# Attention into an ELU feed-forward layer: the first 64 queries of a pair of heads as float16 halves turned by a DMA

## The chip, the cores and the metric

The kernel runs on one core of a Trainium2 chip. The metric is device time in microseconds, the median of several executions. Engines are named as the profile names them: PE is TensorE (PEld its weight loads), DVE VectorE, ACT ScalarE, POOL GpSimd, SP SyncE, which issues all loads and stores.

## The reference

```python
scores = (1/8) * q @ k.T                        # batch 8, heads 8, sequence 576, head size 64
cum    = cumsum(max(s, 0))
scores = where(causal, -1e9, scores + min(-(cum_i - cum_j), 0))
attn   = softmax(scores)
x      = (attn @ v), heads side by side         # 4608 x 512
h      = x @ w_in                               # 512 x 2048
g      = where(h > 0, h, exp(min(h, 0)) - 1)
out    = g @ w_out                              # 4608 x 512, float32
```

## The kernel before, in words

Attention and the feed-forward layer run interleaved in one program. The sequence of 576 queries is cut into the first 64 and four blocks of 128 (`NQ` = 4, `HB` = 64). Heads are worked on in pairs: four pairs in each of the eight batches. The order of the work is: batches 0 to 2, the first 64 queries and blocks 0 and 1, in float32 (class `Low`); batch 3, the same queries, in float16 parts; batches 4 to 7, all queries; at last batches 0 to 3, blocks 2 and 3. The feed-forward layer takes the results in chunks of 256 rows, 18 in all, the first in float32 and the others as products of float16 parts (`moe_chunk`).

Where an operand is split, it is a scaled float16 high part and a float16 rest; a product is three matmuls: high by high, rest by high, high by rest.

A `Unit` is one step of attention. For the five batches 3 to 7 each pair of heads has three units: `h` = None, which does the first 64 queries of both heads at once (one block of 128 x 128: 64 queries of either head against 64 keys of either head, the cross blocks masked away), then `h` = 0 and `h` = 1 for the blocks of each head. So there are 20 units with `h` = None. The pairs of the last batches 0 to 3 have none.

Before, a unit with `h` = None goes like this. `prepare` rounds the 64 values of both heads to float32r and takes the rest (L416, L437). `scoring` makes the scores, the exponentials and their sums (L1065, L1068, L1073), and `normalize` multiplies by the inverse sum (L1086 to L1090). `weighing` turns the block on PE (L1218), copies it out of PSUM in two float32r parts (L443 or L444, L1151) and multiplies both with the values (L1211, two matmuls of 128 columns). The result has 128 rows (high and rest of the values) that are added up by `halves`: for each head a copy (L443 or L444) and an addition (L1280), into the columns 0 to 63 of the tile `x`.

The units with `h` = 0 and 1 do the same for their blocks with float16 parts: `halved` scales the probabilities into a high part and a rest (L1125 to L1133), a transposing DMA (`turned_load`, L409) turns them, and the products of the two heads are issued together after the second (`heads`, L1252). Each of these matmuls has 64 columns of values as weights (128*64 in the profile) and writes one half of the rows of the PSUM bank `av`, head 0 one half and head 1 the other. One eviction with a scale brings the bank into `x` (L1264 on ACT or L1266 on DVE), and a store takes `x` to `x_dram`, from where the feed-forward chunks load it (L404).

PSUM has eight banks: two of the tag "a" (scores and turned blocks), one "av", three "h" and one each of "o0" and "o1" for the feed-forward layer. `any_bank` asks for a bank of "a" or "av". The tile `x` has one buffer (`N_X` = 1).

The order on every engine is written by a planner (`Plan`). An operation lists the engines that could do it with an estimated cost each, what it reads and what it writes. `issue` takes again and again the operation that could start first by the estimates (the smaller priority number in a tie) and puts it on the engine where it would end first. The order is then fixed: each engine executes its instructions in that order, whatever the true durations are. For a buffer with several possible banks it takes the bank that came free earliest:

```python
for key, bufs, *rule in b.others:
    other = slot_free(key, bufs)
    if other is not None and (at is None or other < at):
        at, b.key, b.bufs = other, key, bufs
```

Of the kernel before, what the change touches and what calls it, by code (L numbers as in the profile page):

```python
# [8 lines left out]

F32 = mybir.dt.float32  # L10
F32R = mybir.dt.float32r
U32 = mybir.dt.uint32
BF16 = mybir.dt.bfloat16
F16 = mybir.dt.float16
# [3 lines left out]
P = 128  # L18
# [337 lines left out]
def kernel(  # L356
# [52 lines left out]
        op(prio, [("SP", SP_TURN, lambda: nc.sync.dma_start_transpose(dst(), src()), LAG,  # L409
                   units * P * P * 2)], reads, writes)  # L410

    def rounded(prio, n, dst, src, reads, writes, sign=1.0, only=None):

        ways = [
            ("Pool", pool_1(n),
             lambda: pool.tensor_scalar(dst(), src(), sign, 1.0, ALU.mult, ALU.mult)),  # L416
            ("ACT", act_s(n),
             lambda: act.activation(dst(), src(), AF.Copy, scale=sign)),
            ("DVE-SB", dve_1(n),
             lambda: dve.tensor_scalar(dst(), src(), sign, None, ALU.mult)),  # L420
        ]
        op(prio, [w for w in ways if only is None or w[0] in only], reads, writes)

    def scaled(prio, n, dst, src, by, reads, writes):

        op(prio, [
# [3 lines left out]
            ("DVE-SB", 220 + 0.7 * n, lambda: dve.tensor_scalar(dst(), src(), by(), None, ALU.mult)),  # L430
        ], reads, writes)

    def rest(prio, n, dst, src, hi, reads, writes, only=None):

        ways = [
            ("DVE-SB", dve_2(n), lambda: dve.tensor_tensor(dst(), src(), hi(), ALU.subtract)),
            ("Pool", pool_2(n), lambda: pool.tensor_tensor(dst(), src(), hi(), ALU.subtract)),  # L437
        ]
        op(prio, [w for w in ways if only is None or w[0] in only], reads, writes)

    def psum_copy(prio, n, dst, src, reads, writes, only=None):
        ways = [
# [578 lines left out]
    def prepare(u):  # L1021

        if u.h == 1 or (u.h == 0 and not u.blocks[0]):
            return
        turn = pairs_seen[0] % 2
        pairs_seen[0] += 1
        if len(pair_sets) == turn:
            pair_sets.append(plan.buf(sb, [P, 4, 2, S], F16, "set_1", tag=w_all[1].key[1]))
        if pairs_seen[0] <= 2:
            weigh(pair_sets[turn])  # L1030
        u.set = pair_sets[turn]
        prepare_pair(u, u.set)
        if u.h is not None:
            return
        b, j, prio = u.b, u.j, u.prio
        u.vs = plan.buf(sb, [P, 1, 2, D], F32R, f"vs_{u.tag}", tag="vs0", bufs=NP)
        if u.col == 4:
            prio = PRIO_V
        src, used = (lambda: u.va.v[:, j, :1]), values_of(u.va, j)
        rounded(prio, D, lambda: u.vs.v[:, :1, 0], src, used, [u.vs])  # L1040
        rest(prio, D, lambda: u.vs.v[:, :1, 1], src,
             lambda: u.vs.v[:, :1, 0].bitcast(F32), used, [u.vs])

    plan.signal = (id(ps), "o0")

# [99 lines left out]
            turned_load(prio, turns, lambda: u.pt.v[:, at::n][:, :turns],  # L1145
                        lambda: t16.v[:, base * P : (base + turns) * P], used, [(u.pt, i)])

    def split_pt(prio, tag, tr, w):
        pc = plan.buf(sb, [P, 2, w], F32R, f"pc_{tag}", tag="pc")
        psum_copy(prio, w, lambda: pc.v[:, 0], lambda: tr.v[:, :w], [tr], [(pc, 0)])  # L1150
        op(prio, [("DVE", dve_p(w), lambda: dve.tensor_tensor(  # L1151
            pc.v[:, 1], tr.v[:, :w], pc.v[:, 0].bitcast(F32), ALU.subtract))],
           [tr, (pc, 0)], [(pc, 1)])
        return [(pc, 0), (pc, 1)]

    def scoring(u):

        prio = u.prio
# [5 lines left out]
        used = [(o, part) for part in ("top", "low", "q2", "aux", "weights")]  # L1164
        if u.h is None:
            sm = plan.buf(sb, [P, 1], F32, f"sm_{u.tag}", tag="sm", bufs=2)
            psh = u.pp = plan.buf(sb, [P, P], F32, f"psh_{u.tag}", tag="pc")

            def pair():
                softmax_block(  # L1170
                    prio, u.tag, False, psh, P, masks,
                    lambda at, w: masks.v.rearrange("p h t -> p (h t)"), used,
                    lambda at, w: [
                        (row(q, S - HB, 2 * HB), row(k, u.first, 2 * (S - u.first)).rearrange(
                            "p (h t) -> p h t", h=2)[:, :, :HB]) for q, k in ((Q1, K1), (Q2, K2))],
                    (sm, 0, True, 1, 1.0), view=lambda v: v.rearrange("p (h t) -> p h t", h=2),
                )
                normalize(prio, psh, P, sm, 0)

            return [pair]  # L1180
        c0 = HB * (u.blocks[0] == 0)
# [21 lines left out]
    def weighing(u):  # L1203

        prio = u.prio + 1
        av = plan.buf(ps, [P, 512], F32, f"av_{u.tag}", tag="av", bufs=N_AV)

        def products(cost, pairs, dst, first, last):

            for m, (reads, operands) in enumerate(pairs):  # L1210
                op(prio, [("PE", cost, lambda m=m, operands=operands: pe_.matmul(  # L1211
                    av.v[:, dst], *operands(), start=first and m == 0,
                    stop=last and m == len(pairs) - 1))], reads, [av])

        if u.h is None:
            def pair():
                tr = plan.buf(ps, [P, 512], F32, f"tr_{u.tag}", tag="a", bufs=N_A)
                op(prio, [("PE", 111.0, lambda: pe_.transpose(tr.v[:, :P], u.pp.v, ident))],  # L1218
                   [(u.pp, "data")], [tr])
                pieces = split_pt(prio, u.tag, tr, P)  # L1220
                products(pe(P), [
                    ([pc, u.vs], lambda pc=pc, m=m: (
                        u.vs.v.rearrange("p n a d -> p n (a d)")[:, 0], pc[0].v[:, m]))
                    for m, pc in enumerate(pieces)], slice(P), True, True)
                for h in range(2):
                    halves(prio, h, HB, u.x_part((h, 0)), 0, av, h * HB)

            return [pair]

        if u.h == 0:  # L1230
            return []
        pair = (u.first_head, u)
        first, last, wq = u.blocks[0], u.last + 1, P * u.n_blocks

        def columns(kb):
            i0, half = max(kb - 1, first), kb > first
            return P * (last - i0) - HB * half

        def part(w, kb, m):
            c = columns(kb)  # L1240
            if kb == last:
                return w.pt.v[:, 0, P - c :]
            end = (1 + (2 * kb + m + 1) * w.n_blocks) * P
            return w.pt.v.rearrange("p u q -> p (u q)")[:, end - c : end]

        def heads():
            def step():
                for kb in range(last + 1):
                    dst = slice(wq - columns(kb), wq)
                    for m, v in ((0, 0), (1, 0), (0, 1)) if kb < last else ((0, 0), (0, 1)):  # L1250
                        for w in pair:
                            pe_.matmul(  # L1252
                                av.v[w.h * HB : (w.h + 1) * HB, dst], w.values.v[:, w.h, kb, v], part(w, kb, m),
                                start=kb == 0 and m == 0 and v == 0, stop=kb == last and v == 1,
                            )
# [5 lines left out]
            x, label = u.x_part(("rows", first))  # L1261
            back, cols = slice(u.back, u.back + 1), slice(HB + P * first, HB + P * first + wq)
            op(prio, [
                ("ACT", act_c(wq) + 90, lambda: act.activation(  # L1264
                    x.v[:, cols], av.v[:, :wq], AF.Copy, scale=scales.v[:, back])),
                ("DVE", dve_p(wq), lambda: dve.tensor_scalar(  # L1266
                    x.v[:, cols], av.v[:, :wq], scales.v[:, back], None, ALU.mult)),
            ], [av, (scales, u.back)], [(x, label)])
# [5 lines left out]
    def halves(prio, h, n, dst, c0, av, a0):  # L1274

        x = dst[0]
        own, other = slice(h * HB, (h + 1) * HB), slice((1 - h) * HB, (2 - h) * HB)
        cols, here = slice(c0, c0 + n), slice(a0, a0 + n)
        psum_copy(prio, n, lambda: x.v[own, cols], lambda: av.v[other, here], [av], [dst])
        op(prio, [("DVE", dve_p(n), lambda: dve.tensor_tensor(  # L1280
            x.v[own, cols], av.v[own, here], x.v[own, cols], ALU.add))], [av], [dst])

    def attention():

# [15 lines left out]
        for u, prepared, scored, weighed in todo:  # L1300
# [5 lines left out]
            if type(u) is Unit and u.h is not None:  # L1306
# [1 line left out]
                    pair = pair_values(u, *values)  # L1308
                u.values, u.back = pair, values[1] + 1
                if u.h == 0:  # L1310
                    first_head = u
                u.first_head = first_head
            prepared(u)
            if type(u) is Unit and not hasattr(u, "set"):
                u.set, u.first = operands
# [337 lines left out]
```

## Time and profile before

| | |
|---|---|
| median of 3 runs | 1038.81 us (1037.28 to 1039.48) |
| the profiled execution | 1034.6 us, span 1032.8 us |
| mean granted clock of PE | 0.996 |
| busy PE, PEld | 1003.1 us (97%), 688.7 us (67%) |
| busy DVE, ACT, POOL | 845.2 us (82%), 669.0 us (65%), 295.9 us (29%) |
| transposing DMAs | 168 |
| half-width matmuls (L1252) | 960 |
| float32 turns and products of the first 64 queries (L1218, L1211) | 20 and 40 |

The span is from the first to the last instruction. A busy time is the union of an engine's instructions. Matmuls overlap in the profile, so what one adds to the time of PE is read from the distance of the starts, not from its duration. In a row of a group the last numbers are busy us, mean ns of one, and then the idle time just before with what ended it.

### The profile page before, as it was taken

Reading aid. Unit: us, or ns where it says so; the run is one execution under the profiler, and the core shown is the slowest. Engines: PE = TensorE matmul, PEld = TensorE weight load, DVE = VectorE, ACT = ScalarE, POOL = GpSimd, SP = SyncE. Lnnn points to the kernel's source line nnn. Section 1 sums busy time; section 2 is a strip of 40 time slices with the busy share of each in tenths; the row PEclk is TensorE's granted clock in tenths of the full one; section 3 lists DMA queues with packets and bytes.
Section 4 is the critical chain, followed back from the end, with each engine's and each line's share of the span. In section 5 each row is a group of like instructions: output and inputs, shape, how many; then the busy total and the mean of one; then the engine's idle time right before and its main releaser. Section 6 shows DMA issues by size and latency. Waiting matters only on the chain. (4 is left out here: it accounts for less than half of the span.)

```text
span 1032.8 us, 21782 instructions
## 1 busy us (share of the span) xinstructions
PE 1003.1 (97%) x7305; PEld 688.7 (67%) x7305; DVE 845.2 (82%) x2346; ACT 669.0 (65%) x1559; POOL 295.9 (29%) x487
## 2 busy tenths in 40 slices
PE   8889999999999999999999999999999999999998
PEld 6667656676666666666666666676666676666665
DVE  7999998788988988898889999798988898863232
ACT  4898755666667766776776766666675765644343
POOL 6343452242323323241234242222232123100000
PEclk9999999999999999999999999999999999999999
DMA  7997524589979997999989987979998998841000
GB/s 197 276 289 236 150 72 95 124 190 213 222 166 212 207 192 165 198 202 208 196 174 201 232 179 174 229 181 192 215 198 196 227 202 187 182 94 47 1 21 21
DMA packets 296724, 179.83 MB, mean 174 GB/s; under 512 B 209908, under 2 KB 270564, under 8 KB 296612
## 3 DMA queue, kind: packets, MB, share of 16 engines
q1 hardware_dynamic: 296612, 178.45, 75.7%
q8 instruction: 57, 0.93, 0.4%
q14 instruction: 55, 0.45, 0.2%
HBM read 93.08 MB, written 36.81 MB: 126 GB/s over the span
## 5 line engine op out<-in xcount | busy, mean ns | idle before, releaser
L1427 PE MATMUL h<-xh,wp 128*128 128x256 f16 x2176 | 402.7, 273 | 0.7 <-DVE gg L1466 0.7
L1484 PE MATMUL o<-wp,gg 128*128 128x512 f16 x1632 | 392.7, 380 | 0.5 <-DVE gg L1466 0.5
L1427 PEld LDWEIGHTS <-wp 128*128 128x128 f16 x3264 | 317.4, 98 | 69.7 <-issue 2.1
L1427 PE MATMUL h<-xl,wp 128*128 128x256 f16 x1088 | 297.3, 273 | 1.1 <-DVE xl L1403 1.1
L1484 PEld LDWEIGHTS <-gg 128*128 128x128 f16 x1632 | 157.7, 98 | 144.5 <-DVE gg L1466 1.0
L1073 ACT ACTIVATE p<-p,mn 128x192 f32<-128x192 f32 (+1 forms) x232 | 143.7, 620 | 54.9 <-DVE mn L1068 52.9
L1133 DVE SCALAR_TENSOR_TENSOR p<-p,sm,p 128x512 f16<-128x512 f32 (+3 forms) x257 | 162.8, 662 | 4.9 <-POOL p L1125 2.4
L1459 DVE SCALAR_TENSOR_TENSOR h<-g,cs,h 128x512 f32<-128x512 f32 x136 | 102.0, 750 | 60.5 <-ACT g L1446 59.2
L1125 POOL TENSOR_SCALAR p<-p,sm 128x512 f16<-128x512 f32 (+3 forms) x94 | 65.1, 696 | 290.5 <-DVE sm L1079 117.1
L1439 ACT ACTIVATE g<-h,cs 128x512 f32<-128x512 f32 x136 | 92.8, 682 | 78.0 <-PE h L1427 77.2
L1463 ACT ACTIVATE gg<-h 128x512 f16<-128x512 f32 x132 | 78.3, 593 | 83.2 <-DVE h L1459 79.3
L1068 DVE CUSTOM_DVE_ANT_0 p<-sc,maskw 128x192 f32<-128x192 f32 (+1 forms) x232 | 109.5, 481 | 11.9 <-PE sc L1065 8.5
L1065 PE MATMUL sc<-set 128*128 128x288 f16 (+3 forms) x544 | 112.7, 299 | 4.5 <-DVE mn L1068 4.3
L1466 DVE SCALAR_TENSOR_TENSOR gg<-h,gg 128x512 f16<-128x512 f32 x136 | 93.3, 686 | 16.3 <-ACT gg L1463 15.7
L1129 ACT ACTIVATE p<-p,sm 128x512 f16<-128x512 f32 (+3 forms) x139 | 75.1, 557 | 19.0 <-DVE sm L1079 5.5
L1065 PEld LDWEIGHTS <-set 128*128 128x128 f16 x584 | 55.1, 98 | 41.6 <-issue 8.6
L1252 PE MATMUL av<-T,v 128*64 128x256 f16 (+5 forms) x960 | 62.4, 278 | 2.8 <-DMA T<-p 2.8
L1252 PEld LDWEIGHTS <-v 128*64 128x64 f16 x960 | 48.5, 110 | 23.3 <-issue 12.3
L1446 ACT ACTIVATE g<-g 128x512 f32<-128x512 f32 x81 | 50.9, 628 | 1.9
L428 POOL TENSOR_SCALAR v<-va,scales 128x320 f16<-128x320 f32 (+1 forms) x45 | 26.8, 599 | 64.9 <-PE av L1252 58.3
L1073 ACT ACTIVATION_READ_ACCUMULATOR p<-p,mn 128x1 f32 x232 | 43.7, 188 | 0.0
L1068 DVE CUSTOM_DVE_ANT_0 p<-sc,maskw,mn 128x288 f32<-128x288 f32 x64 | 32.9, 514 | 7.1 <-PE sc L1065 5.5
(200 smaller groups left out, 1261.0 us busy)
## 6 DMA issues: line engine op xcount, KB each, us to landing
set<-spread SPq DMA_DIRECT2D x32, 432.0 KB
spread<-parts_None SPq DMA_DIRECT2D x32, 288.0 KB
set<-spread SPq DMA_DIRECT2D x32, 288.0 KB
raws<-in_w_in_dram SPq DMA_DIRECT2D x16, 512.0 KB
raws<-in_w_out_dram SPq DMA_DIRECT2D x16, 512.0 KB
out_dram<-ost SPq DMA_DIRECT2D x32, 256.0 KB
va<-in_vb_dram SPq DMA_DIRECT2D x16, 352.0 KB
xc<-x_dram SPq DMA_DIRECT2D x22, 256.0 KB
```

Of the source, the lines that this page charges most:

```text
L1065: pe_.matmul(view(sc.v[:, :cw]), l, r, start=n == 0, stop=n == len(pairs) - 1)
L1068: op(prio, [("DVE", 84 + dve_p(cw), lambda i=i, sc=sc: dve.tensor_tensor_reduce(pt.v[:, i * cw : (i + 1) * cw], sc.v[:, :cw], mv(i * cw, c ...
L1073: op(prio, [("ACT", 480 + w / 1.2, lambda: act.activation(pt.v[:, :w], pt.v[:, :w], AF.Exp, bias=mn.v[:, n - 1 : n], scale=-1.0, accum_out ...
L1129: ("ACT", 295 + size / 1.2, lambda part=part: act.activation(part(0), own(part), AF.Copy, scale=sm.v[:, r])),
L1133: ("DVE-SB", dve_2(size), lambda part=part: dve.scalar_tensor_tensor(part(1), own(part), sm.v[:, r], part(0), ALU.mult, ALU.subtract)),
L1252: pe_.matmul(av.v[w.h * HB : (w.h + 1) * HB, dst], w.values.v[:, w.h, kb, v], part(w, kb, m), start=kb == 0 and m == 0 and v == 0, stop=kb ...
L1427: pe_.matmul(columns(k), weight_part(f, 0, part)[1]()[:, c * P : (c + 1) * P], xx.v[:, c], start=(c == 0 and m == 0), stop=(c == NCB - 1 a ...
L1439: op(side, [("ACT", act_c(W) + (0 if native else 90), lambda: act.activation(g.v, hp.v, AF.Exp, scale=1.0 if native else by(3)))], [hp] + ...
L1459: op(side, [("DVE", dve_p(W), lambda: dve.scalar_tensor_tensor(hp.v, g.v, by(2 if sign[0] else 1), hp.v, ALU.mult, ALU.max))], [g, cs], [hp])
L1463: ("ACT", act_c(W), lambda: act.activation(gg.v[:, 0], hp.v, AF.Copy, scale=2.0**-DOWN)),
L1466: op(side, [("DVE", dve_p(W), lambda: dve.scalar_tensor_tensor(gg.v[:, 1], hp.v, 2.0**-DOWN, gg.v[:, 0], ALU.mult, ALU.subtract))], [hp, ( ...
L1484: pe_.matmul(acc[i].v, gg.v[:, g, at], weight_part(f, 1, part)[1](), start=(f == 0 and m == 0), stop=(f == NF - 1 and m == 2),)
```

## The change

For the 20 units with `h` = None:

- The values are split into float16 parts by the scale of the batch's group, as those of the other blocks are (`split_scaled`), in place of the two float32r parts.
- The normalized probabilities are written as a float16 high part and a rest (`split_scaled` on 128 columns), and a DMA turns both (`turned_load`, 2 units of 128 x 128). They have tiles of their own (`psh`, `ph`, `th`) where they shared the tag "pc" before.
- The turn on PE, its copies, the two products and `halves` are gone. The unit has no step of its own in `weighing` any more.
- The products are now part of `heads`, after the second head: `front_step`, six matmuls of 64 columns with half-width weights, head 0 and head 1 in turn. For batch 3 (two blocks, 256 columns) they go into the first 64 columns of the same bank as the heads' products, and one eviction takes all 320 columns. For batches 4 to 7 (four blocks, 512 columns, a full bank) they go into a bank from `any_bank` and are evicted by an instruction of their own.
- `front_step` reads its own turned block and lists the turned blocks of both heads as inputs too.

```diff
+    def split_scaled(prio, n, dst, src, by, used, parts):
+        scaled(prio, n, lambda: dst(0), src, by, used, [(parts, 0)])
+        op(prio, [("DVE-SB", dve_2(n), lambda: dve.scalar_tensor_tensor(
+            dst(1), src(), by(), dst(0), ALU.mult, ALU.subtract))], [*used, (parts, 0)], [(parts, 1)])
...
-        u.vs = plan.buf(sb, [P, 1, 2, D], F32R, f"vs_{u.tag}", tag="vs0", bufs=NP)
+        u.vs = plan.buf(sb, [P, 2, D], F16, f"vs_{u.tag}", tag="vs0", bufs=NP)
...
-        rounded(prio, D, lambda: u.vs.v[:, :1, 0], src, used, [u.vs])
-        rest(prio, D, lambda: u.vs.v[:, :1, 1], src,
-             lambda: u.vs.v[:, :1, 0].bitcast(F32), used, [u.vs])
+        by = lambda: scales.v[:, u.col : u.col + 1]
+        split_scaled(prio, D, lambda m: u.vs.v[:, m], src, by, used, u.vs)
...
-            psh = u.pp = plan.buf(sb, [P, P], F32, f"psh_{u.tag}", tag="pc")
+            psh = plan.buf(sb, [P, P], F32, f"psh_{u.tag}", tag="psh")
+            p16 = plan.buf(sb, [P, 2, P], F16, f"ph_{u.tag}", tag="ph")
+            u.pt = plan.buf(sb, [P, 2, P], F16, f"th_{u.tag}", tag="th", bufs=2)
...
-                normalize(prio, psh, P, sm, 0)
+                split_scaled(prio, P, lambda m: p16.v[:, m], lambda: psh.v, lambda: sm.v[:, :1],
+                             [sm, (psh, "data")], p16)
+                turned_load(prio, 2, lambda: u.pt.v, lambda: p16.v.rearrange("p m q -> p (m q)"),
+                            [(p16, 0), (p16, 1)], [u.pt])
...
-        if u.h is None:
-            def pair():
-                tr = plan.buf(ps, [P, 512], F32, f"tr_{u.tag}", tag="a", bufs=N_A)
-                op(prio, [("PE", 111.0, lambda: pe_.transpose(tr.v[:, :P], u.pp.v, ident))],
-                   [(u.pp, "data")], [tr])
-                pieces = split_pt(prio, u.tag, tr, P)
-                products(pe(P), ...)
-                for h in range(2):
-                    halves(prio, h, HB, u.x_part((h, 0)), 0, av, h * HB)
...
+        front = u.front if not first else None
+        c0 = HB * (front is not None and wq + HB <= 512)
...
+            if front is not None:
+                fav = av if c0 else any_bank(f"avh_{u.tag}")
+                def front_step():
+                    for m, v in ((0, 0), (1, 0), (0, 1)):
+                        for h in range(2):
+                            pe_.matmul(
+                                fav.v[h * HB : (h + 1) * HB, :HB], front.vs.v[:, v], front.pt.v[:, m, h * HB : (h + 1) * HB],
+                                start=m == 0 and v == 0, stop=v == 1,
+                            )
+                op(prio, [("PE", 120.0, front_step)], [front.pt, *[(w.pt, i) for w in pair for i in u.blocks],
+                                                       (front.vs, 0), (front.vs, 1)], [fav])
+                if not c0:
+                    evicted(HB, lambda: x.v[:, :HB], lambda: fav.v[:, :HB], [fav], [(x, "first")])
```

More of the change, by code (lines that the diff above doesn't have):

```diff
@@ L10 @@
 F32 = mybir.dt.float32
-F32R = mybir.dt.float32r
 U32 = mybir.dt.uint32
@@ L410, in turned_load @@
                    units * P * P * 2)], reads, writes)
[L412 to L422, printed above, removed]
     def scaled(prio, n, dst, src, by, reads, writes):
@@ L431, in scaled @@
         ], reads, writes)
[L433 to L439, printed above, removed]
+    def split_scaled(prio, n, dst, src, by, used, parts):
+        scaled(prio, n, lambda: dst(0), src, by, used, [(parts, 0)])
+        op(prio, [("DVE-SB", dve_2(n), lambda: dve.scalar_tensor_tensor(
+            dst(1), src(), by(), dst(0), ALU.mult, ALU.subtract))], [*used, (parts, 0)], [(parts, 1)])
     def psum_copy(prio, n, dst, src, reads, writes, only=None):
@@ L1035, in prepare @@
         b, j, prio = u.b, u.j, u.prio
-        u.vs = plan.buf(sb, [P, 1, 2, D], F32R, f"vs_{u.tag}", tag="vs0", bufs=NP)
+        u.vs = plan.buf(sb, [P, 2, D], F16, f"vs_{u.tag}", tag="vs0", bufs=NP)
         if u.col == 4:
             prio = PRIO_V
-        src, used = (lambda: u.va.v[:, j, :1]), values_of(u.va, j)
-        rounded(prio, D, lambda: u.vs.v[:, :1, 0], src, used, [u.vs])
-        rest(prio, D, lambda: u.vs.v[:, :1, 1], src,
-             lambda: u.vs.v[:, :1, 0].bitcast(F32), used, [u.vs])
+        src, used = (lambda: u.va.v[:, j, 0]), [*values_of(u.va, j), (scales, u.col)]
+        by = lambda: scales.v[:, u.col : u.col + 1]
+        split_scaled(prio, D, lambda m: u.vs.v[:, m], src, by, used, u.vs)
     plan.signal = (id(ps), "o0")
@@ L1146, in halved @@
                         lambda: t16.v[:, base * P : (base + turns) * P], used, [(u.pt, i)])
[L1148 to L1154, printed above, removed]
     def scoring(u):
@@ L1175, in pair @@
                             "p (h t) -> p h t", h=2)[:, :, :HB]) for q, k in ((Q1, K1), (Q2, K2))],
-                    (sm, 0, True, 1, 1.0), view=lambda v: v.rearrange("p (h t) -> p h t", h=2),
+                    (sm, 0, True, 1, UP), view=lambda v: v.rearrange("p (h t) -> p h t", h=2),
                 )
-                normalize(prio, psh, P, sm, 0)
+                split_scaled(prio, P, lambda m: p16.v[:, m], lambda: psh.v, lambda: sm.v[:, :1],
+                             [sm, (psh, "data")], p16)
+                turned_load(prio, 2, lambda: u.pt.v, lambda: p16.v.rearrange("p m q -> p (m q)"),
+                            [(p16, 0), (p16, 1)], [u.pt])
             return [pair]
@@ L1205, in weighing @@
         prio = u.prio + 1
[L1206 to L1213, printed above, removed]
-        if u.h is None:
-            def pair():
-                tr = plan.buf(ps, [P, 512], F32, f"tr_{u.tag}", tag="a", bufs=N_A)
-                op(prio, [("PE", 111.0, lambda: pe_.transpose(tr.v[:, :P], u.pp.v, ident))],
-                   [(u.pp, "data")], [tr])
-                pieces = split_pt(prio, u.tag, tr, P)
[L1221 to L1224, printed above, removed]
-                for h in range(2):
-                    halves(prio, h, HB, u.x_part((h, 0)), 0, av, h * HB)
-            return [pair]
-        if u.h == 0:
+        if u.h != 1:
             return []
         pair = (u.first_head, u)
+        av = plan.buf(ps, [P, 512], F32, f"av_{u.tag}", tag="av", bufs=N_AV)
         first, last, wq = u.blocks[0], u.last + 1, P * u.n_blocks
+        front = u.front if not first else None
+        c0 = HB * (front is not None and wq + HB <= 512)
         def columns(kb):
@@ L1246, in heads, with evicted @@
         def heads():
+            x, label = u.x_part(("rows", first))
+            back = slice(u.back, u.back + 1)
+            def evicted(n, dst, src, reads, writes):
+                op(prio, [
+                    ("ACT", act_c(n) + 90, lambda: act.activation(dst(), src(), AF.Copy, scale=scales.v[:, back])),
+                    ("DVE", dve_p(n), lambda: dve.tensor_scalar(dst(), src(), scales.v[:, back], None, ALU.mult)),
+                ], [*reads, (scales, u.back)], writes)
+            if front is not None:
[11 more added lines that the diff above has]
+                    evicted(HB, lambda: x.v[:, :HB], lambda: fav.v[:, :HB], [fav], [(x, "first")])
             def step():
                 for kb in range(last + 1):
-                    dst = slice(wq - columns(kb), wq)
+                    dst = slice(c0 + wq - columns(kb), c0 + wq)
                     for m, v in ((0, 0), (1, 0), (0, 1)) if kb < last else ((0, 0), (0, 1)):
@@ L1260, in heads @@
                [av])
[L1261 to L1268, printed above, removed]
+            cols = slice(HB + P * first - c0, HB + P * first + wq)
+            evicted(c0 + wq, lambda: x.v[:, cols], lambda: av.v[:, : c0 + wq], [av], [(x, label)])
             load(prio, lambda: x_dram.v[u.b, u.j][:, u.cols], lambda: x.v[:, u.cols], [x],
@@ L1272, in weighing @@
         return [heads]
[L1274 to L1281, printed above, removed]
     def attention():
@@ L1310, in attention @@
                 if u.h == 0:
-                    first_head = u
+                    first_head, u.front = u, None if u.blocks[0] else front
+                u.front = first_head.front
                 u.first_head = first_head
+            if type(u) is Unit and u.h is None:
+                front = u
             prepared(u)
```

## The prediction

> **What bounds the kernel.** I read the page's busy shares first, then the busy time by stretch, then TensorE's waits behind 100 us, because a change that takes work from four engines is worth only what the bounding one gets.
>
> ```profile
> span 1032.8 us, 21782 instructions
> PE 1003.1 (97%) x7305; PEld 688.7 (67%) x7305; DVE 845.2 (82%) x2346; ACT 669.0 (65%) x1559; POOL 295.9 (29%) x487
> ```
> ```profile
> 125.00:150.00 25.00, 24.60 (x85) 15.36 (x84) 24.59 (x55) 15.53 (x31) 14.37 (x14) 1.00 0.19 66
> 150.00:175.00 25.00, 22.87 (x148) 15.47 (x147) 23.39 (x65) 14.41 (x33) 9.56 (x14) 0.93 0.25 65
> 187.00:618.00 431.00, 424.38 (x3206) 289.62 (x3205) 385.00 (x1119) 302.50 (x727) 144.63 (x219) 1.00 0.91 194
> ```
> ```profile
> PE sc L1065 <- DVE mn L1068: 4.3, 9, 0.9
> PE av L1252 <- DMA T<-p: 2.8, 3, 1.8
> PE tr_None L1218 <- ACT psh_None L1090: 2.1, 1, 2.1
> PE tr_None L1218 <- POOL psh_None L1086: 1.5, 2, 0.8
> PE av_None L1211 <- ACT x_None L1264: 0.6, 1, 0.6
> PE av_None L1211 <- DVE x_None L1266: 0.3, 1, 0.3
> ```
>
> The columns of the second fence are the stretch, its length, busy PE, PEld, DVE, ACT and POOL with their counts, the granted clock, the DMA share and GB/s. From 187 to 618 us, where nearly all the changed steps stand, TensorE is busy 424.4 of 431 us and VectorE 385: TensorE bounds, and idles 6.6 us there. So the change is worth what it takes from TensorE's own work, plus the waits in which TensorE's fixed order holds it. Of the waits behind 100 us (third fence: total us, count, longest), 3.6 us stand before the turn of the first 64 queries (L1218) and 0.9 us before its products (L1211): 4.5 us in five waits, at instructions that the change deletes. The other two rows are waits that it leaves.
>
> The span is 1032.8 us in an execution of 1034.6 us; the median of the runs is 1038.81, 4.2 us above it. I sum differences in the profiled execution and put them on the median.
>
> **TensorE's work, per pair of heads (20 of them).** Removed: one float32 turn and two products of 128 columns. What each adds to the stream is read from start to start, in three places without a wait:
>
> ```profile
> 616.62 1.46 PE L1484 MATMUL o<-wp,gg 128*128 128x512 f16 x6
> 617.92 0.27 PE L1218 MATMUL tr_None<-ident,psh_None 128*128 128x128 f32 x1
> 618.03 1.46 PE L1484 MATMUL o<-wp,gg 128*128 128x512 f16 x6
> ```
> ```profile
> 299.48 0.27 PE L1427 MATMUL h<-xl,wp 128*128 128x256 f16 x1
> 299.59 0.27 PE L1427 MATMUL h<-xh,wp 128*128 128x256 f16 x1
> 299.62 0.42 PE L1211 MATMUL av_None<-pc_None,vs_None 128*128 128x128 f32 x2
> 299.88 0.28 PE L1427 MATMUL h<-xh,wp 128*128 128x256 f16 x1
> ```
> ```profile
> 181.09 0.27 PE L1427 MATMUL h<-xl,wp 128*128 128x256 f16 x1
> 181.20 0.27 PE L1427 MATMUL h<-xh,wp 128*128 128x256 f16 x1
> 181.40 0.83 PE L1252 MATMUL av<-T,v 128*64 128x256 f16 x16
> 182.16 0.28 PE L1427 MATMUL h<-xh,wp 128*128 128x256 f16 x1
> ```
>
> The turn takes 618.03 - 617.92 = 0.11 us. The two products push the next L1427 from 299.70 (299.59 plus the 0.11 us of one) to 299.88: 0.18 us. Together 0.29 us, times 20: 5.8 us go.
>
> Added: six half-width matmuls of 64 columns, in pairs side by side. The step at 181.40 shows the price of this form. Its 16 matmuls are 8 pairs and stream 3 x 256 + 3 x 192 + 2 x 64 = 1472 columns. At the rate of L1427 (256 columns in 0.11 us) that is 0.63 us. It takes 182.16 - 181.31 = 0.85 us, so 0.22 us are the way into and out of half width. Three pairs of 64 columns stream 192 columns, 0.08 us. Directly beside a heads step (L1252) the front is worth 0.08 us, standing alone 0.30.
>
> Which of the two? For the four pairs of batch 3 the front shares the bank of the heads' products and has the same inputs, so it stands beside them: 4 x 0.08 = 0.3 us. For the other 16 it asks for any bank of the tags "a" and "av", and the planner takes the one free for longest. The two "a" banks turn over with every score block, "av" has been idle since the last pair. So the front takes "av", and the heads' products can be placed only when it has been evicted; other matmuls go between, and the front pays 16 x 0.30 = 4.8 us. Work: -5.8 + 0.3 + 4.8 = **-0.7 us**; with all 20 beside the heads it would be -5.8 + 1.6 = -4.2. I take -0.7, from the planner's rule.
>
> The Trainium skill, "TensorEngine Tiling (Array Packing)", Key Properties, says that changing the tiling mode drains TensorE; it gives no figure. The 0.22 us above is what this trace shows of it, and it is why narrower products are no cheaper here unless they stand together.
>
> **Waits of TensorE that go.** The front now waits for what the heads wait for as well, and its own turned block was issued long before theirs. What the five waits held back is then later work. Four of them (2.4 us of 4.5) stand in the long stretch where TensorE is the bound: I take all of it, -2.4. The first, 2.1 us at 155.0, is followed by a lower clock: 0.93 over 25 us is 1.75 us lost. But VectorE was busy 24.59 of the 25 us ahead of it with the weights' parts that TensorE needs next, and the change moves four values splits into that time, since they now need the group's scale. So I take half of 2.1 + 1.75: -1.9. Together **-4.3 us**, ends 0 (all of it comes back as waits for VectorE) and -6.3.
>
> The Trainium skill, "TensorE: Matmul & The Clock Gate", What's actually happening, has the clock fall after an idle window of about 3.4 us. The row has a clock of 0.93 beside one wait of 2.1 us. By the page this wait alone would not cost the clock; the sum would be 0.9 us higher.
>
> **A wait that is added.** In 16 pairs the heads' products wait for the front's eviction from "av". The nearest rows are L1211 behind the eviction of the same bank: 0.6 + 0.3 us in 20 pairs, 0.045 us each. 16 x 0.045 = **+0.7 us**; ends 0 and 16 x 0.6 = 9.6.
>
> **The other engines.**
>
> ```profile
> L1151 DVE TENSOR_TENSOR pc_None<-tr_None,pc_None 128x128 fp32r<-128x128 f32 x20 | 5.6, 282 | 0.5 <-ACT pc_None L443 0.5
> L1280 DVE TENSOR_TENSOR x_None<-av_None,x_None 64x64 f32<-64x64 f32 x40 | 8.8, 219 | 1.2 <-ACT x_None L443 0.5
> L444 DVE COPY x_None<-av_None 64x64 f32<-64x64 f32 x17 | 3.8, 221 | 3.3 <-DMA x_dram<-x_None 2.1 <-ACT x_None L443 0.8
> L444 DVE CAST pc_None<-tr_None 128x128 fp32r<-128x128 f32 x5 | 1.4, 283 | 0.8 <-PE tr_None L1218 0.8
> L443 ACT CAST pc_None<-tr_None 128x128 fp32r<-128x128 f32 x15 | 3.9, 259 | 2.9 <-PE tr_None L1218 2.8
> L443 ACT COPY x_None<-av_None 64x64 f32<-64x64 f32 x23 | 4.7, 206 | 2.0 <-DMA x_dram<-x_None 1.4
> L437 POOL TENSOR_TENSOR vs_None<-va,vs_None 128x64 fp32r<-128x64 f32 x19 | 8.0, 425 | 2.1 <-ACT vs_None L418 1.2
> ```
> ```profile
> L1133 DVE SCALAR_TENSOR_TENSOR p<-p,sm,p 128x64 f16<-128x64 f32 x50 | 15.0, 301 | 2.0 <-POOL p L1125 1.4 <-ACT p L1129 0.4
> L1133 DVE SCALAR_TENSOR_TENSOR p<-p,sm,p 128x256 f16<-128x256 f32 x47 | 26.0, 561 | 0.8 <-POOL p L1125 0.6
> L1264 ACT ACTIVATE x<-av,scales 128x256 f32<-128x256 f32 x8 | 3.7, 466 | 1.6 <-PE av L1252 1.6
> ```
>
> VectorE loses 5.6 + 8.8 + 3.8 + 1.4 = 19.6 us, ScalarE 3.9 + 4.7 = 8.6, GpSimd the 8.0 of L437. VectorE gains 20 subtracts of 128 columns (between 0.301 and 0.561 us, by the columns 0.39: 7.8 us) and 20 of 64 (6.0 us); 16 evictions of 64 columns (below the 0.466 us of 256; about 0.3, 4.8 us) go to it or to ScalarE. Scaling the probabilities and the values' high part replaces an instruction of the same size. So VectorE gains between 1 and 6 us of free time in 845. It is not the bound: 0 us on the path. It is also the cover of the first term: were VectorE later, the 2.4 us would not come.
>
> The queue of loads gets 20 turning transfers, each behind the subtract of its block:
>
> ```profile
> L409 SPq DMA_TRANSPOSE T<-p x168: 1206/1309/4601, 172.6 to 922.4; - x168
> SPq L409 <- DVE mn L1068: 36.9, 32, 2.6
> SPq L409 <- DVE p L1133: 32.6, 27, 4.5
> ```
>
> 20 x 1.31 = 26 us of its time, and what is queued behind each are the next pair's loads, for which the score products (L1065) wait. From 187 to 618 us these two rows alone (its largest waits) hold 69 us of waiting, so the 26 us have room: 0 us, at most +2.8, a second time the 2.8 us that TensorE waits for turned blocks. The buffer x is now taken at the heads and no longer at the first 64 queries, which only ends the waits for x_dram in L444 and L443 above: 0.
>
> **Sum:** -0.7 - 4.3 + 0.7 = -4.3 us; 1038.8 - 4.3 = **1034.5 us**, 0.4% faster.
>
> **The rivals.** (1) The fronts stand beside the heads in all pairs and every wait goes: -4.2 - 6.3 = -10.5, 1028.3 us. Against it: the rule for banks above. (2) The reordered plan makes as many waits as it removes. The 4.3 us of L1065 behind VectorE in nine places show that such waits arise wherever the plan's durations are off. Only the work is left: -0.7, 1038.1 us, no difference. (3) Slower: the heads' products meet the front's eviction in "av". VectorE is 89% busy there, so the eviction often stands behind another instruction, and TensorE, whose order is fixed, idles. At the longest wait of that bank, 0.6 us, in all 16 pairs: +9.6 - 0.7 - 4.3 = +4.6, 1043.4 us. It decides from (0.7 + 4.3) / 16 = 0.31 us a pair; for it speaks that this bank did stop TensorE twice, against it that it did so in 2 of 20.
>
> **How the numbers follow.** Forecast 0.47, rival 1 0.15, rival 2 0.2, rival 3 0.18. 0.2% (2 us) is about what a measurement of this kernel can tell from no change. Faster is the forecast and rival 1 (0.62), same rival 2 (0.2), slower rival 3 (0.18). The likeliest case alone reaches from 1031.5 to 1036.5. For 8 in 10 the range goes up between the deciding point and rival 3 and down nearly to rival 1: 1029 to 1041.5.
>
> **What would show it.** Right: no TensorE wait at L1218 or L1211, 120 new half-width matmuls of 64 columns, the 16 fronts of full groups standing among L1427 or L1484 and not next to the heads, waits of TensorE for evictions of "av" under 1 us in sum, granted clock 1.00 from 150 to 175 us. Wrong: fronts beside the heads (then faster); heads' products idling behind evictions, or L1065 behind loads of "set" (then slower); a wait of 2 us for VectorE near 155 us in place of the one removed (then the same).

## The result and the profile after

The changed kernel takes 1046.24 us (median of 10 runs, 1042.53 to 1051.68) against 1038.05 us (10 runs) before: 1.0085 times the time, with a 95% interval of 1.0065 to 1.0105. It is 0.85% slower, above the range that was forecast. The profiled execution took 1046.02 us, its span 1044.2 us.

The page of the changed kernel, its span and the busy engines:

```profile
span 1044.2 us, 21827 instructions
PE 1004.6 (96%) x7365; PEld 685.4 (66%) x7365; DVE 841.6 (81%) x2328; ACT 666.5 (64%) x1534; POOL 248.4 (24%) x424
```

TensorE is busy 1.5 us longer (1003.1 before), with 60 matmuls more (20 times six for 20 times three). It stands idle for 1044.2 - 1004.6 = 39.6 us, where it was 1032.8 - 1003.1 = 29.7 us. So 9.9 of the 11.4 us by which the span grew are idle time, and the question is what TensorE waits for. Its waits in the whole span (total us, times, longest), after:

```profile
PE sc L1049 <- DVE mn L1052: 9.2, 17, 1.3
PE av L1237 <- DMA T<-p: 6.5, 5, 2.9
PE h L1400 <- ACT xh L416: 2.9, 1, 2.9
PE h L1400 <- DVE xl L1376: 1.2, 1, 1.2
```

and before, for the score products (L1065 there):

```profile
PE sc L1065 <- DVE mn L1068: 5.7, 12, 1.0
```

The waits of L1218 and L1211 are gone with their instructions. In their place the score products wait 3.5 us more for VectorE, the heads' products 3.7 us more for turned blocks (2.8 us before), and the feed-forward products (L1400) 4.1 us in two waits; before, none of theirs was over 0.7 us. These two stand close together. Of the 6.5 us of the heads' products, 2.9 us are one wait at 845 us. Stretches of the changed kernel (length, busy PE, PEld, DVE, ACT, POOL with counts, granted clock, DMA share, GB/s):

```profile
150.00:175.00 25.00, 22.16 (x141) 14.38 (x140) 24.60 (x65) 13.38 (x29) 6.63 (x9) 1.00 0.20 56
350.00:400.00 50.00, 44.12 (x326) 28.91 (x323) 41.48 (x125) 30.77 (x74) 11.12 (x16) 0.93 0.91 202
```

and the second of them before:

```profile
350.00:400.00 50.00, 49.53 (x369) 33.91 (x368) 44.57 (x137) 33.50 (x81) 14.58 (x23) 1.00 0.97 205
```

The clock near 155 us is whole now. The waiting there is not less, though: in the 25 us TensorE idles 2.8 us (25 - 22.16), where it was 2.1 us, now in two waits for results of VectorE (`gg`, 1.6 and 1.2 us). Between 350 and 400 us TensorE is 5.4 us less busy than before, and at a clock of 0.93, which is another 3.5 us of 50. The timeline of TensorE there (start, duration, in brackets the idle time ahead and who ended it):

```profile
362.57 0.43 PE L1049 MATMUL sc<-set 128*128 128x320 f16 x2 [0.54 <-DVE mn_None L1052]
365.95 0.37 PE L1400 MATMUL h<-xh,wp 128*128 128x256 f16 x1 [2.95 <-ACT xh L416]
367.51 0.37 PE L1400 MATMUL h<-xl,wp 128*128 128x256 f16 x1 [1.19 <-DVE xl L1376]
368.11 0.42 PE L1400 MATMUL h<-xl,wp 128*128 128x256 f16 x1
```

L1400 waits for the operand of a feed-forward chunk, the first rows of batch 4, and then runs at half speed (0.42 us where its mean is 0.27; the granted clock is 0.50 from 366 to 370 us and 1.00 again from 375 us). In this order of the plan the feed-forward layer has run ahead of attention. So there are two candidates for the loss: the order that the planner now writes, and something that the change itself costs in any order.

The work of the first 64 queries came as forecast. The instructions on the bank `avh` (min, median and longest ns), and one front of a full group in the timeline:

```profile
L1222 PE MATMUL avh<-th_None,vs_None x96: 196/196/217, 275.8 to 662.8; 128*64 128x64 f16 x96
```
```profile
349.56 0.27 PE L1400 MATMUL h<-xh,wp 128*128 128x256 f16 x1
349.76 0.28 PE L1222 MATMUL avh<-th_None,vs_None 128*64 128x64 f16 x6
349.98 0.45 PE L1049 MATMUL sc<-set 128*128 128x320 f16 x2
```

The front stands alone, away from the heads. From 349.67 (349.56 plus the 0.11 us of one L1400) to 349.98 it takes 0.31 us, against 0.30 in the prediction. The other 15 stand alone too and take the same.

### The profile page after: what moved, and what is told of

Its sections match the earlier page's. It is cut to its first block, busy times and chain, and to the rows that moved or that the text cites. A ratio compares the mean times of both kernels' runs of the same rounds, so it can differ in the third digit from the quotient of the medians.

```text
span 1044.2 us, 21827 instructions
## 1 busy us (share of the span) xinstructions
PE 1004.6 (96%) x7365; PEld 685.4 (66%) x7365; DVE 841.6 (81%) x2328; ACT 666.5 (64%) x1534; POOL 248.4 (24%) x424
## 5 line engine op out<-in xcount | busy, mean ns | idle before, releaser
L1400 PE MATMUL h<-xh,wp 128*128 128x256 f16 x2176 | 399.0, 273 | 4.4 <-ACT xh L416 2.9
L1400 PEld LDWEIGHTS <-wp 128*128 128x128 f16 x3264 | 317.7, 98 | 71.6 <-issue 6.9
L1400 PE MATMUL h<-xl,wp 128*128 128x256 f16 x1088 | 297.2, 273 | 1.2 <-DVE xl L1376 1.2
L1117 DVE SCALAR_TENSOR_TENSOR p<-p,sm,p 128x512 f16<-128x512 f32 (+3 forms) x260 | 159.0, 640 | 6.3 <-POOL p L1109 3.2
L1052 DVE CUSTOM_DVE_ANT_0 p<-sc,maskw 128x192 f32<-128x192 f32 (+1 forms) x232 | 108.5, 480 | 9.3 <-PE sc L1049 6.4
L1113 ACT ACTIVATE p<-p,sm 128x512 f16<-128x512 f32 (+3 forms) x133 | 72.3, 559 | 25.4 <-DMA T<-p 7.5
L1237 PE MATMUL av<-T,v 128*64 128x256 f16 (+5 forms) x960 | 64.2, 281 | 6.7 <-DMA T<-p 6.5
L1237 PEld LDWEIGHTS <-v 128*64 128x64 f16 x960 | 49.6, 111 | 27.5 <-issue 17.2
L1052 DVE CUSTOM_DVE_ANT_0 p<-sc,maskw,mn 128x288 f32<-128x288 f32 x64 | 32.8, 512 | 7.6 <-PE sc L1049 6.7
```

The costliest lines, as they stand in the source:

```text
L1052: op(prio, [("DVE", 84 + dve_p(cw), lambda i=i, sc=sc: dve.tensor_tensor_reduce(pt.v[:, i * cw : (i + 1) * cw], sc.v[:, :cw], mv(i * cw, c ...
L1113: ("ACT", 295 + size / 1.2, lambda part=part: act.activation(part(0), own(part), AF.Copy, scale=sm.v[:, r])),
L1117: ("DVE-SB", dve_2(size), lambda part=part: dve.scalar_tensor_tensor(part(1), own(part), sm.v[:, r], part(0), ALU.mult, ALU.subtract)),
L1237: pe_.matmul(av.v[w.h * HB : (w.h + 1) * HB, dst], w.values.v[:, w.h, kb, v], part(w, kb, m), start=kb == 0 and m == 0 and v == 0, stop=kb ...
L1400: pe_.matmul(columns(k), weight_part(f, 0, part)[1]()[:, c * P : (c + 1) * P], xx.v[:, c], start=(c == 0 and m == 0), stop=(c == NCB - 1 a ...
```

## The experiments

Two theories went into them. **The order:** the plan came out unlucky, and the change costs nothing by itself. **The queue:** the 20 turning transfers cost SyncE time for which the loads behind them come late. A third, that VectorE's added subtract of 128 columns is what is late, was tested on the side.

### One planner's cost raised by 1 ns

These kernels compute the same with the same instructions. Only one cost that the planner assumes is 1 ns higher, so that another order comes out. Four such edits were made to the kernel after and to the kernel before alike:

```diff
 def dve_p(n):
-    return 155 + 1.04 * n          # dve1
+    return 156 + 1.04 * n
 ...
-    return 160 + 1.06 * n          # sub1
+    return 161 + 1.06 * n
 ...
-    return 165 + n / 1.2           # act1
+    return 166 + n / 1.2
 ...
-    return 120 + 1.04 * n          # pool1
+    return 121 + 1.04 * n
```

> The changed kernel with one number of the planner raised by 1 ns (its estimate of a VectorE instruction on PSUM, 155 to 156), so that it writes another order of the same instructions. Theory 'order' (the 8 us come from the order that the planner happened to write: TensorE ran ahead of attention and stood still at 361 to 368 us, behind the load of the first chunk of batch 4): by the planner's own sums this order ends 9 us earlier, so about 1037 us, and no wait of TensorE for xh longer than 1 us. Rival 'own cost' (the turning transfers, the bank of the front and the extra VectorE work slow attention in every order): 1046 us within 2.

> The changed kernel with the planner's estimate of a VectorE subtraction raised by 1 ns (160 to 161). Theory 'order': the planner's own sum ends 8 us earlier, about 1038 us. Rival 'own cost': 1046 us within 2.

> The changed kernel with the planner's estimate of a ScalarE instruction on PSUM raised by 1 ns (165 to 166). Theory 'order': the planner's own sum ends 9 us later, about 1055 us. Rival 'own cost': 1046 us within 2.

> The changed kernel with the planner's estimate of a GpSimd instruction raised by 1 ns (120 to 121). Theory 'order': the planner's own sum ends 3 us earlier, about 1043 us. Rival 'own cost': 1046 us within 2.

> The kernel before with the planner's estimate of a VectorE instruction on PSUM raised by 1 ns (155 to 156). Theory 'order': orders of the kernel before scatter as those of the changed one do; the planner's own sum for this one is unchanged within 0.5 us: 1038 us. Rival 'own cost': 1038 us within 2, as all orders of this kernel.

> The kernel before with the planner's estimate of a VectorE subtraction raised by 1 ns (160 to 161). Theory 'order': the planner's own sum is unchanged within 0.5 us: 1038 us. Rival 'own cost': 1038 us within 2.

> The kernel before with the planner's estimate of a ScalarE instruction on PSUM raised by 1 ns (165 to 166). Theory 'order': the planner's own sum ends 5 us later: about 1043 us. Rival 'own cost': 1038 us within 2.

> The kernel before with the planner's estimate of a GpSimd instruction raised by 1 ns (120 to 121). Theory 'order': the planner's own sum ends 9 us later: about 1047 us, as slow as the changed kernel. Rival 'own cost': 1038 us within 2.

Measured, as ratios to the kernel before (interval in brackets) and medians:

| costs | kernel before | kernel after | after over before |
|---|---|---|---|
| as given | 1 | 1.0085 [1.0065, 1.0105], 1046.24 | +0.85% |
| dve1 | 0.9916 [0.9894, 0.9937], 1028.92 | 0.9982 [0.9965, 0.9999], 1035.68 | +0.66% |
| sub1 | 0.9947 [0.9929, 0.9965], 1031.98 | 1.0034 [1.0018, 1.0050], 1039.80 | +0.87% |
| pool1 | 1.0007 [0.9989, 1.0025], 1039.16 | 1.0056 [1.0040, 1.0073], 1042.93 | +0.49% |
| act1 | 1.0050 [1.0024, 1.0076], 1043.67 | 1.0155 [1.0130, 1.0179], 1053.25 | +1.05% |

Each kernel moves by 1.3 to 1.7% from best to worst when nothing but the order changes. That is more than the whole effect in question, and with another order the changed kernel can even come out a little ahead of the given kernel before (after_dve1). So the order matters as the first theory says. The planner's own sums foretold the four new orders of the kernel after to 2 us, but of those of the kernel before only act1: they missed dve1, sub1 and pool1 by 6 to 9 us. But with the same costs the changed kernel is behind in all five pairs, by 0.49 to 1.05%, 0.78% on average: the change has a cost of its own too. In every pair TensorE waits longer for VectorE at the score products: 8.1 to 17.8 us in the five orders after, 0.2 to 5.7 before. A theory of the order alone falls. (The planner writes different orders for the two kernels even then. The runs that follow hold the order fixed.)

### The turning transfer left out, copied plainly, doubled

These keep the changed kernel's order to the instruction. The first does not issue the 20 transfers, and the products of the first 64 queries read a tile of zeros. The second also cuts the subtract of the probabilities' rest to 4 of 128 columns. The third copies the two blocks without turning them. The fourth issues each turning transfer twice, the second time into a spare tile.

```diff
-                turned_load(prio, 2, lambda: u.pt.v, lambda: p16.v.rearrange("p m q -> p (m q)"),
-                            [(p16, 0), (p16, 1)], [u.pt])
+                op(prio, [("SP", SP_TURN, lambda: None, LAG, 2 * P * P * 2)], [(p16, 0), (p16, 1)], [u.pt])   # no_turn
 ...
+                op(prio, [("DVE-SB", dve_2(P), lambda: dve.scalar_tensor_tensor(                             # no_turn_narrow
+                    p16.v[:, 1, :4], psh.v[:, :4], sm.v[:, :1], p16.v[:, 0, :4], ALU.mult, ALU.subtract))],
 ...
+                op(prio, [("SP", SP_TURN, lambda: nc.sync.dma_start(u.pt.v, p16.v), LAG, 2 * P * P * 2)],      # plain_copy
+                   [(p16, 0), (p16, 1)], [u.pt])
 ...
+                def twice():                                                                                # turn_twice
+                    for to in (u.pt.v, again):
+                        nc.sync.dma_start_transpose(to, p16.v.rearrange("p m q -> p (m q)"))
```

> The changed kernel in exactly its own order, with the 20 turning transfers of the first 64 queries left out: the planner still counts them, so every engine has the same instructions in the same places, and the products read a block of zeros (the output of the first 64 queries of batches 3 to 7 is left out). In five orders the changed kernel was slower than the kernel before in the same order of costs, by 0.5 to 1.0%, and TensorE waited 8 to 18 us at the scores for VectorE's minimum where it waited 2 to 6 us. Theory 'queue' (the 20 transfers, 1.2 us each in the queue of loads, make the next pair's loads and turned blocks land late; VectorE and ScalarE stand behind these, and TensorE behind them): about 7 us come back, 1039 us against 1046. Rival 'VectorE' (the 40 subtracts on VectorE, longer than the planner counts, are what is late): 1046 us within 2.

> As no_turn, and the subtract that makes the rest of the probabilities works on 4 of 128 columns (the rest is left out; in the same place of the same order): 20 x 0.2 us less of VectorE. Theory 'queue': no faster than no_turn by more than 1 us. Rival 'VectorE': this one is the faster, by 4 us or more.

> The changed kernel in exactly its own order, with the 20 turning transfers made as plain copies of the same 64 KB from and to the same tiles (the turning is left out). SyncE still waits for the subtract at each, but spends about 0.6 us and not 1.2. Theory 'queue': about half of what no_turn gains, 3 to 4 us, 1042 us; if the turning itself is what costs, all of it, 1039 us; if the wait for the subtract at the head of the queue is what costs, nothing, 1046 us. Rival 'VectorE': 1046 us.

> The changed kernel in exactly its own order, with each of the 20 turning transfers issued a second time, into a tile that nothing reads. Theory 'queue': another 20 x 1.2 us in the queue of loads, 5 to 8 us slower, 1052 us. Rival 'VectorE': 1046 us within 2.

| kernel | median us | ratio to before |
|---|---|---|
| no_turn | 1035.94 | 0.9998 [0.9979, 1.0016] |
| no_turn_narrow | 1036.23 | 0.9997 [0.9983, 1.0012] |
| plain_copy | 1040.93 | 1.0037 [1.0022, 1.0052] |
| after (one transfer) | 1046.24 | 1.0085 [1.0065, 1.0105] |
| turn_twice | 1061.17 | 1.0234 [1.0210, 1.0259] |

Without the transfers the kernel is level with before: 1.0085 - 0.9998 = 0.0087, 9 us. The shorter subtract (0.22 us each in place of 0.34) gives nothing on top, so VectorE's subtract of the probabilities is not the cause, as far as kernels without the transfers can tell. Twice the transfers cost 0.0149, 15 us, more, where 5 to 8 us were expected. The plain copy, with the same bytes, saves about half. The issue rows of the transfer on SyncE (min, median and longest ns), in the kernel after and in plain_copy:

```profile
L408 SPq DMA_TRANSPOSE th_None<-ph_None x20: 1167/1202/1517, 167.4 to 632.3; - x20
```
```profile
L1158 SPq DMA_DIRECT2D th_None<-ph_None x20: 511/542/1217, 166.8 to 627.0; - x20
```

The pages of no_turn, plain_copy and turn_twice, in this order:

```profile
span 1034.0 us, 21787 instructions
PE 1003.8 (97%) x7365; PEld 685.5 (66%) x7365; DVE 840.6 (81%) x2328; ACT 667.0 (65%) x1534; POOL 250.0 (24%) x425
```
```profile
span 1035.9 us, 21827 instructions
PE 1000.9 (97%) x7365; PEld 683.1 (66%) x7365; DVE 842.8 (81%) x2328; ACT 665.9 (64%) x1534; POOL 249.2 (24%) x424
```
```profile
span 1057.7 us, 21856 instructions
PE 1009.6 (95%) x7365; PEld 686.6 (65%) x7365; DVE 842.5 (80%) x2328; ACT 665.8 (63%) x1534; POOL 250.0 (24%) x424
```

TensorE's idle time in these executions, span less busy, is 30.2, 35.0, (after) 39.6 and 48.1 us, while SyncE's added issue time, from the median issue, is 0, 20 x 0.54 = 11, 20 x 1.20 = 24 and about 48 us. TensorE idles some 0.4 us more for each us that SyncE issues, whether the transfer turns or not. The wait of its score products for VectorE follows: 9.2 us in the kernel after (shown above), and in no_turn and turn_twice:

```profile
PE sc L1051 <- DVE mn L1054: 3.7, 8, 1.0
```
```profile
PE sc L1050 <- DVE mn L1053: 15.8, 18, 2.8
```

How it reaches TensorE is seen where one pair's turn stands ahead of a later pair's loads. SyncE's timeline of no_turn, then after, then turn_twice, from the same `T` transfer on:

```profile
315.99 5.30 SPq L408 DMA_TRANSPOSE T<-p  x4
321.38 1.87 SPq L403 DMA_DIRECT2D set<-spread  x3
323.29 1.23 SPq L403 DMA_DIRECT2D stk_None<-in_kT_dram  x2
324.62 2.54 SPq L403 DMA_DIRECT2D stq_None<-in_qT_dram  x4
```
```profile
316.93 5.37 SPq L408 DMA_TRANSPOSE T<-p  x4
322.75 1.20 SPq L408 DMA_TRANSPOSE th_None<-ph_None  x1
324.00 1.86 SPq L403 DMA_DIRECT2D set<-spread  x3
325.90 1.24 SPq L403 DMA_DIRECT2D stk_None<-in_kT_dram  x2
327.24 2.53 SPq L403 DMA_DIRECT2D stq_None<-in_qT_dram  x4
```
```profile
320.60 5.37 SPq L408 DMA_TRANSPOSE T<-p  x4
326.06 1.21 SPq L1161 DMA_TRANSPOSE th_None<-ph_None  x1
327.32 1.24 SPq L1161 DMA_TRANSPOSE again<-ph_None  x1
328.62 1.87 SPq L403 DMA_DIRECT2D set<-spread  x3
330.53 1.23 SPq L403 DMA_DIRECT2D stk_None<-in_kT_dram  x2
331.86 2.53 SPq L403 DMA_DIRECT2D stq_None<-in_qT_dram  x4
```

From the end of the `T` transfers the load of `stq` starts after 3.33, 4.94 and 5.89 us. Between the turn and that load SyncE has no gap in which the turn could hide: the loads simply slide. (In the kernel after 0.4 us of the slide are a gap ahead of the turn; what it waits for there is not shown.) It is so for most: 16 of the 20 turns start within 0.15 us of the end of the transfer before them, and the other four stand at 323 us and before. What follows in the changed kernel, on all engines:

```profile
333.65 0.75 DVE L608 TENSOR_REDUCE pk_None<-stq_None 128x1 f32<-128x576 f32 x1 [2.58 <-DMA stq_None<-in_qT_dram]
334.32 0.61 DVE L1052 CUSTOM_DVE_ANT_0 p<-sc,maskw 128x448 f32<-128x448 f32 x1
334.99 0.41 PE L1049 MATMUL sc<-set 128*128 128x288 f16 x2 [0.65 <-DVE mn L1052]
```

VectorE stands 2.58 us for `stq`. The minimum of a score block (L1052), which only stands behind that reduction in VectorE's order, comes late, its bank is not free, and TensorE idles 0.65 us. This is why the profile names VectorE as the releaser, though the delay came from SyncE. At the same place VectorE stands 0.70 us for `stq` in no_turn, and no wait of TensorE follows; in turn_twice it stands 4.01 us, and TensorE idles 2.09 us behind it. ScalarE does such reductions as well. It waits 3.3, 6.6 and 18.4 us for that load in no_turn, after and turn_twice. That row alone does not measure the cost, though: it is 7.1 us in plain_copy and 7.5 us in the kernel before.

### What of a transfer costs

The first of these turns a tile of zeros, so that SyncE has no wait for the subtract but issues the same. The second turns only one of the two blocks: half the bytes.

```diff
+                op(prio, [("SP", SP_TURN, lambda: nc.sync.dma_start_transpose(                # turn_of_zeros
+                    u.pt.v, still.rearrange("p m q -> p (m q)")), LAG, 2 * P * P * 2)], [(p16, 0), (p16, 1)], [u.pt])
 ...
+                op(prio, [("SP", SP_TURN, lambda: nc.sync.dma_start_transpose(                # turn_half
+                    u.pt.v[:, :1], p16.v[:, 1]), LAG, 2 * P * P * 2)], [(p16, 0), (p16, 1)], [u.pt])
```

> The changed kernel in exactly its own order, where each of the 20 transfers turns a standing tile of zeros (the probabilities of the first 64 queries are left out): the same issue and bytes, but SyncE need not wait for the subtract. Theory 'issue' (SyncE's 1.2 us each delay all loads queued behind): 1046 us within 2. Rival 'wait' (the queue stands at its head for the subtract): 1038 us. Rival 'bytes': 1046.

> The changed kernel in exactly its own order, where each of the 20 transfers turns only the rest of the probabilities, 32 KB and not 64 (the products read it for both parts, so the high part is left out). Theory 'issue': SyncE's time for it hardly depends on the size (1.21 us at the least for the blocks' transfers of two to nine times the bytes), so 1045 us within 2. Rival 'bytes': half of the 9 us, 1041 us.

Measured: turn_of_zeros 1044.02 us, 1.0074 [1.0054, 1.0094]; turn_half 1042.74 us, 1.0072 [1.0048, 1.0096]. Both are within the error of the change (1.0085), some 0.3 points, and far from no_turn (0.9998). So the wait of SyncE for the subtract is not the main cost. Nor are the bytes, as far as one transfer's half can tell. A smaller share of either stays possible: in the profiled execution of turn_of_zeros TensorE idles 35.0 us (span 1041.7, busy 1006.7), between no_turn and after. Issuing half the bytes takes as long:

```profile
L1158 SPq DMA_TRANSPOSE th_None<-ph_None x20: 1121/1189/1809, 167.4 to 633.0; - x20
```

### The turns joined to transfers that are there anyway

If issues cost, fewer should be cheaper. For the 16 pairs of batches 4 to 7 the two blocks of the first 64 queries are written into unused columns of the tile that the first transfer of head 0 turns, and go with it. This is the whole computation, and only the four transfers of batch 3 stay separate. The plan is a new one, once with the costs as given and once with those of dve1.

```diff
+            units = 2 * u.turns[i + 1] - 1 if joint else turns + u.turns[i + 1] + 2 * (front is not None)
 ...
+        if front is not None:
+            first, by = base + turns, lambda: front.sm.v[:, :1]
 ...
+            used += [high, low]
+            front.at, front.step, turns = at + n * turns, n, turns + 2
```

> The whole computation, with the probabilities of the first 64 queries split later, beside block 0 of the first head, and turned by that block's transfer (16 of the 20 transfers go, the bytes stay; batch 3 keeps its own). The order is the planner's own for it. Theory 'issue' or 'wait': 7 us less than the changed kernel for the queue, and by the planner's own sum 2.5 us less for the order: about 1037 us. Rival 'bytes': 1044 us.

> As joined, with the planner's estimate of a VectorE instruction on PSUM raised by 1 ns, the order in which both kernels were at their fastest (0.992 of the kernel before for the unchanged one, 0.998 for the changed one). Theory 'issue' or 'wait': 7 us less than the changed kernel in that order, about 1028 us, level with the unchanged kernel in that order. Rival 'bytes': 1035 us.

Measured: joined 1032.53 us, 0.9962 [0.9938, 0.9986]; joined_dve1 1028.14 us, 0.9928 [0.9903, 0.9953]. The first is 4.5 us below what was expected, the second as expected. With the same costs that is 1.2% below the change as given and 0.5% below after_dve1. Both orders beat both kernels as given; against before_dve1 (0.9916) the second is level. Of the joined kernel, the page, the issues, and TensorE's waits:

```profile
span 1028.4 us, 21819 instructions
PE 1001.1 (97%) x7365; PEld 684.3 (67%) x7365; DVE 833.7 (81%) x2318; ACT 668.1 (65%) x1538; POOL 247.7 (24%) x437
```
```profile
L408 SPq DMA_TRANSPOSE T<-p x168: 1192/1314/4365, 172.7 to 918.8; - x168
L408 SPq DMA_TRANSPOSE th_None<-ph_None x4: 1170/1208/1303, 166.2 to 229.3; - x4
```
```profile
PE sc L1049 <- DVE mn L1052: 4.6, 8, 1.1
PE av L1254 <- DMA T<-p: 3.0, 4, 1.2
```

The two blocks ride for nothing that could be seen: added up from the timeline, with the short gaps between neighbours, the 168 transfers of `T` hold SyncE for about 312 us in this kernel and in the one after alike. 16 issues are gone, and both waits are back to about their size before. TensorE's idle time is 27.3 us. Since the order changes too, two orders do not say how much of the gain the issues have alone. The experiments with the order held fixed do.

## Why the prediction was wrong

**The step that failed is the queue of loads.** It was costed at 0, at most +2.8 us, because SyncE's two largest waits held 69 us "so the 26 us have room". The 20 transfers cost 9 us, and their removal alone brings the time back. The 26 us of issue time were about right (20 x 1.20 = 24). What was wrong is the reading of the waits. SyncE issues in the planned order: a wait of its queue takes up added work only if it stands between the added work and the load that is late, and at 322 us above there is none. Nor does the delay come mainly by the way that the prediction names: from no_turn to after TensorE's own wait for `set` grows from 0.9 to 1.4 us, but its wait for VectorE at the scores from 3.7 to 9.2. The two rows of waits that the prediction adds up, over the whole span of no_turn, after and turn_twice:

```profile
SPq L408 <- DVE p L1119: 67.4, 38, 5.1
SPq L408 <- DVE mn L1054: 41.7, 31, 3.7
```
```profile
SPq L408 <- DVE p L1117: 55.1, 34, 5.2
SPq L408 <- DVE mn L1052: 36.7, 30, 3.5
```
```profile
SPq L408 <- DVE p L1118: 39.3, 23, 5.1
SPq L408 <- DVE mn L1053: 36.1, 31, 3.5
```

In sum 109.1, 91.8 and 75.4 us: some 17 us go out of them for each 24 us added. The rest made loads late, although 75 us of waiting were still left. The joined kernel has 76.3 us in these rows and is faster than all three: their sum alone does not tell the slack.

**The plan's order was taken as otherwise unchanged.** The term of -4.3 us for waits that go came true only in part: the waiting instructions are gone, and the clock is 1.00 from 150 to 175 us. But two waits for VectorE stand there now, as the prediction feared, and the new order made others: the 4.1 us at L1400 with the slow stretch behind them, and 2.9 us at 845 us for a turned block of the other queries. No_turn has all of these as well (2.9 and 1.2, 3.1 us), so they belong to the order and not to the transfer. This is rival 2, and it fits that no_turn ends at 0.9998: by the prediction's own terms, -0.7 and -4.3, it would have ended near 1033. No run takes these waits out one by one, so this part is argued. The prediction gave that rival 0.2, but had no sense of how much an order alone moves this kernel, 1.3 to 1.7%.

**Right:** the fronts' form and place (16 alone at 0.31 us, four beside the heads), so that TensorE's work hardly changes. A shorter subtract on VectorE gains nothing (no_turn_narrow); the work of ScalarE and GpSimd was not tried by itself. None of TensorE's waits in the whole span is for the eviction of "av" (in the order dve1 there are 2.0 us of them), so the +0.7 was too much here, and rival 3, which ended near the measured time, did so for another reason than the one that came true.

**Open:** why the second transfer of turn_twice costs 15 us where the first costs 9. In the profiled executions idle time grows alike, by 9.4 us from no_turn to after and by 8.5 us from there to turn_twice. The second time TensorE is also busy 5.0 us longer, at a granted clock of 0.990 in place of 0.993; the clock makes some 3 us of that (1% of 1057.7 us less 0.7% of 1044.2). Open is also how the cost divides, to within 3 us, between issuing and moving the bytes (the mean DMA share from 400 to 650 us is 0.92 in no_turn, after and turn_twice alike). An issue from another engine's queue was not tried.

## What to carry to other kernels

Waits of an in-order queue are no slack in themselves: look at what is queued right behind the new transfer and whether a wait stands between, or else count its issue time as partly on the path (0.4 here). Blocks that can ride in a transfer that is issued anyway cost less than an issue of their own. Where a planner writes the order, compare a change over several orders, since a cost edit of 1 ns moved this kernel by more than the change did.

## What the runs showed of the hardware

A turning transfer holds SyncE for 1.20 us for 64 KB and 1.19 us for 32 KB, while a plain copy of the 64 KB holds it for 0.54 us. The Trainium skill, "Advanced Engine Details and Errata", X-Bar Transpose (TRN2), says that transposing DMAs are as fast as regular ones. That may hold for the moving of bytes, which no run here separates; for the issue it does not.

TensorE ran at half speed after idling 2.95 us at 363 us, with 0.54 us idle before it: the next L1400 took 0.37 us, those after it 0.42, and the granted clock was 0.67 from 363 to 366 us, 0.50 from 366 to 370. It was 0.57 from 845 to 849 us, behind the wait of 2.87 us at L1237. The Trainium skill, "TensorE: Matmul & The Clock Gate", What's actually happening, speaks of an idle window of about 3.4 us. Here the shorter waits were followed by the lower clock, as 2.1 us were at 155 us in the kernel before.
